# A longer hand-ordered opening: twelve pairs of groups instead of nine, another order behind W', and GpSimd from the fifth unit on

## Chip, cores, metric

The kernel runs on one core of one Trainium2 chip. The metric is the device time in microseconds of one execution. The core has five engines that run their own instruction queues in order: TensorE (PE in the profile, with its weight loads as PEld), VectorE (DVE), ScalarE (ACT), GpSimd (POOL) and SyncE (SP), which here only issues transfers.

## Reference

Three layers are computed one after the other on 2304 tokens:

```python
# q, k, v: (4, 8, 576, 64) float32
out = coarse_attention(mean4(q), mean4(k), mean4(v)) repeated 4 times
    + local_attention(q, k, v)          # |i - j| < 4
x = out as (2304, 512)
x = ((x @ w1) * (x @ w2)) @ w3 @ w_out  # w1, w2: 512x1024, w3: 1024x1024, w_out: 1024x512
h = x @ w_in                            # 512x2048
y = (h * sigmoid(h)) @ w_out2           # 2048x512
```

The weights arrive as float64 and are turned into float32 on the chip, in four integer and float steps per block.

## The kernel before

**Units, groups, slots.** Attention is cut into 16 units (one batch and two heads each). The product with w1 and w2 (called ab) is cut into 9 groups of 256 tokens and 8 blocks m of 128 columns; a pair (g, m) is two slots, one for w1 (w = 0) and one for w2 (w = 1). A slot is 12 matmuls of 128x128 by 128x256, in thirds a, b, c of four. Every three matmuls and every slot's end call `tick()`, so that a slot is four beats. There are 144 slots. Groups 0 and 1 need only units 0 to 3, and are the first 32 slots.

**W'.** w3 and w_out are multiplied into one matrix W' by 64 calls `p<half><gp><q>` of 128x128 by 128x512 in full float32; each is two MATMULs in the trace. Eight copies `wh<half><j>` bring it out of PSUM.

**The opening.** The list `OPENING` holds short names of steps; under `manual_schedule` every engine's queue gets its instructions in the order of that list. What stands there, by name (the last digit is the unit u, or the weight block m behind `w12_`):
- SP: `Lq`, `Lr`, `Lva`, `Lvb` (loads of q and k, of v for the coarse and the local part), `Lww12_m0/1` (weights), `Sc<g><m>` (store of a finished pair to DRAM)
- PE: `sd`, `s` (coarse and local scores), `td`, `tl` (transposes of the two probability tiles), `od`, `ol` (sums with v), `ab<g><m><w><third>`, `p...`
- ACT: `xd`, `x0`..`x2` (exponentials), `cd`, `cl` (copies of the transposes), `xh` (high half of x), `aw`, `hw` (first and fifth step of a weight block), `af` (copy of the first product of a pair), `wh`
- DVE: `md`, `mk`, `ml`, `rd`, `rl` (maxima, mask, inverses), `os`, `xf` (sums out of PSUM), `pq` (sums of q and k by four), `d2`, `d1`, `d3`, `lw` (steps of a weight block), `cf` (product of a pair)
- `nd`, `n0`..`n2` (norms of the probabilities), `pv0`, `pv1` (sums of v by four) and `xo` (low half of x): while `opening[0]` is true the norms run as small multiplications on ACT (line 374) and the others on DVE (lines 503, 510, 579). Behind the opening all of them run on GpSimd (the norm as one instruction, line 376).

PSUM has four banks for ab and W' (`mm`), two for transposes and sums (`T`), two for scores (`S`). `cf` has three buffers, `af` two, q/k, vr and vw two each, the probability tile `band` one, weight stages two.

**Behind the opening** only PE's order is written out by hand: slot after slot, with the units' steps taken from `table` when the beat comes (`TURN[u]`: transposes of u and scores of u+1; `SUMS[u]`: `ol`, x). The order on the other engines is made when the kernel is built. A background list `plan` decodes 16 more weight blocks (`bg_steps`) from slot 26 on, one every 21/4 slots; at its end the stage pools are closed (`open_y`). After slot 143 come the products with W', with w_in and with the last weights, all on PE.

In the version before, the opening ends with slot 17 (nine pairs, beat 72) and unit 6's exponentials; unit 6's turn is at beat 74, its sums at beat 88, unit 7's scores between. From slot 18 to the end of slot 23 (beat 96) three more pairs run under the table.

Of the kernel before, what the change touches and what calls it, by code (L numbers as in the profile page):

```python
# [11 lines left out]
ALU = mybir.AluOpType  # L12
# [3 lines left out]
NU = NB * NHP  # L16
# [36 lines left out]
n20 pv00 ao1 pv10 Lwt030 pq1 s1 cd00 cd10 tl00 tl10 d1o1 Lr1 cl00 sd1 cl10 d3o1 tl20 od0 Lwt031  # L53
cl20 md1 p010 os0 xd1 pq2 p011 Lq3 ao2 p012 d2o2 Lwt100 p013 rd1 mk1 nd1 p014 d1o2 Lwt101 d3o2 sd2
at02 d2t02 s2 Lww12_00 md2 p015 d1t02 p016 Lww12_01 d3t02 ao3 p017 ml1 ol0 Lq4 d1o3 x01 Lwt110 p020
pv01 x11 pv11 p021 d2o3 Lva1 x21 d3o3 p022 at03 p023 rl1 Lr2 d2t03 p024 n01 d1t03 n11 p025 d3t03
Lvb1 n21 p026 pq3 p027 Lwt111 p030 d2t10 at10 xf00 p031 Lww12_20 xf10 xh00 td01 d1t10 xh10 td11
cd01 d3t10 Lww12_21 p032 cd11 xd2 tl01 d2w12_0 tl11 p033 xo00 cl01 rd2 cl11 tl21 xo10 aw12_0 p034
mk2 ml2 od1 cl21 wh00 d1w12_0 p035 nd2 p036 os1 wh01 d3w12_0 p037 x02 ol1 wh02 wh03 pv02 p100 x12
Lva2 Lvb2 p101 x22 xf01 p102 xf11 hw12_0 rl2 td02 pv12 td12 n02 d2t11 Lr3 p103 n12 lw12_0 p104 n22  # L60
d2w12_2 sd3 xh01 xh11 xo01 cd02 s3 xo11 cd12 md3 tl02 at11 Lq5 tl12 pq4 p105 cl02 p106 cl12 aw12_2
d1t11 tl22 d3t11 od2 cl22 xd3 p107 os2 Lwt120 d1w12_2 p110 Lwt121 d3w12_2 sd4 rd3 ol2 Lww12_30
hw12_2 mk3 Lww12_31 ml3 nd3 p111 lw12_2 Lva3 Lvb3 x03 p112 xf02 p113 x13 xf12 pv03 td03 x23 d2t12
# [6 lines left out]
p137 wh12 Lva5 Lvb5 ab000a wh13 rd5 ab000b hw12_1 ab000c ab001a lw12_1 af00 nd5 ab001b ml5 ab001c  # L70
Lr6 ab100a cf00 Sc00 ol4 ab100b x05 xf04 xf14 ab100c xh04 x15 ab101a xh14 af10 x25 xo04 rl5 ab101b
xo14 ab101c ab020a cf10 Sc10 n05 n15 ab020b n25 pv05 ab020c pv15 Lva6 Lvb6 Lr7 ab021a af02 td05
cd05 ab021b td15 cd15 ab021c cf02 Sc02 ab120a pq6 tl05 cl05 ab120b tl15 cl15 ab120c ab121a aw12_5
af12 tl25 ab121b od5 cl25 os5 ab121c cf12 Sc12 ab030a d2w12_5 sd6 md6 ab030b d1w12_5 xd6 ab030c s6
Lq8 rd6 mk6 ab031a af03 ml6 ab031b nd6 d3w12_5 ab031c cf03 Sc03 ab130a x06 hw12_5 Lww12_60 ab130b
x16 lw12_5 Lww12_61 ab130c x26 rl6 ab131a af13 ol5 xf05 xf15 xh05 ab131b n06 n16 xh15 xo05 ab131c
n26 cf13 Sc13 xo15 ab010a aw12_4 d2w12_4 ab010b d1w12_4 ab010c ab011a af01 d3w12_4 ab011b hw12_4
ab011c cf01 Sc01 ab110a lw12_4 Lww12_70 ab110b Lww12_71 ab110c d2w12_6 aw12_6 ab111a af11 ab111b
d1w12_6 ab111c cf11 Sc11 ab050a d3w12_6 ab050b hw12_6 ab050c ab051a lw12_6 af05 ab051b aw12_7
ab051c d2w12_7 cf05 Sc05 d1w12_7 d3w12_7 hw12_7 lw12_7  # L80
""".split()


# [1 line left out]
def tile_model(ctx: ExitStack, tc: tile.TileContext, qk, vw, vr, w12, w3t, wo, wb, out):  # L85
    nc = tc.nc
# [78 lines left out]
    for g in range(4):  # L165
        mv = mask[QW * g:QW * g + QW]
        nc.gpsimd.affine_select(
            out=mv, in_=mv, compare_op=ALU.is_ge, fill=NEG, base=0,
# [3 lines left out]
            out=mv, in_=mv, compare_op=ALU.is_ge, fill=NEG, base=6,  # L172
# [140 lines left out]
    A = {}  # L313
    opening = [True]

    def side():
        return nc.vector if opening[0] else nc.gpsimd

    def load_qk(u):
        t = att.tile([P, 1158], F32, tag="qk", name=f"qk{u}")  # L320
# [29 lines left out]
    def unit_ops(u):  # L350
# [18 lines left out]
            nc.vector.reciprocal(out=sv, in_=sv)  # L369

        def norm(z, E, n, width, lo, hi):
            if opening[0]:
                for j in range(lo, hi):
                    nc.scalar.mul(E[:, j, :], E[:, j, :], z[:, NQB + j:NQB + j + 1])
            elif lo == 0:
                nc.gpsimd.tensor_tensor(
                    out=E, in0=E, op=ALU.mult,
                    in1=z[:, NQB:NQB + n].unsqueeze(2).to_broadcast([P, n, width]),
                )
# [120 lines left out]

        def pool_v0():
            r = A["vr", u][:HD]
            side().tensor_tensor(
                out=r[:, :, 0:2, :], in0=r[:, :, 0:2, :], in1=r[:, :, 2:4, :], op=ALU.add
            )

        def pool_v1():
            r = A.pop(("vr", u))[:HD]
            t = att.tile([HD, 2, P], F32, tag="vd", name=f"vd{u}", bufs=1)
            side().tensor_tensor(out=t, in0=r[:, :, 0, :], in1=r[:, :, 1, :], op=ALU.add)  # L510
            hold["vd"] = t

        def coarse_sums():
# [62 lines left out]

        def x_rest(h):
            for x, xf in x_parts(h):
                side().tensor_tensor(
                    out=x[:, 1], in0=xf, in1=x[:, 0].bitcast(F32), op=ALU.subtract  # L580
                )

# [2 lines left out]
        op("xd" + U, coarse_exps)  # L585
        op("rd" + U, lambda: inverse(hold["zd"], 3, 0.25))
        op("nd" + U, lambda: norm(hold["zd"], hold["Ed"], 3, SD, 0, 3))
        op("s" + U, local_scores)
        op("mk" + U, local_mask)
# [33 lines left out]
                fn()  # L623

    GAP = 4
    SUMS = {6: 88, **{u: 116 + 32 * (u - 7) for u in range(7, 16)}}
    TURN = {6: 74, 7: 102, **{u: SUMS[u] - 22 for u in range(8, 16)}}
    table = {}
    for u in range(6, NU):
        for when, names in (  # L630
            (TURN[u], f"pq{u + 1} td0{u} cd0{u} td1{u} cd1{u}"),
            (TURN[u] + GAP, f"tl0{u} cl0{u} tl1{u} cl1{u}"),
            (TURN[u] + 2 * GAP,
             f"tl2{u} od{u} cl2{u} os{u} pv0{u + 1} pv1{u + 1} sd{u + 1} md{u + 1} xd{u + 1} "
             f"rd{u + 1} nd{u + 1}"),
            (TURN[u] + 3 * GAP,
             f"s{u + 1} mk{u + 1} ml{u + 1} x0{u + 1} x1{u + 1} x2{u + 1} "
             f"rl{u + 1} n0{u + 1} n1{u + 1} n2{u + 1} Lq{u + 3} Lr{u + 3}"),
            (SUMS[u],
             f"ol{u} xf0{u} xh0{u} xo0{u} xf1{u} xh1{u} xo1{u} Lva{u + 2} Lvb{u + 2}"),  # L640
        ):
# [796 lines left out]
    with tc.manual_schedule(engines={E.PE, E.DVE, E.Activation, E.Pool, E.SP}):  # L1438
# [31 lines left out]
        for u in range(NUN):  # L1470
            t, p = divmod(u, 8)
# [98 lines left out]
```

## Time and profile before

| what | value |
|---|---|
| runs, median (lowest to highest) | 803.53 us (803.06 to 805.8), 3 runs |
| the profiled execution: time, span | 798.11 us, 796.3 us |
| PE busy | 784.8 us (99%), 7706 matmuls |
| DVE, ACT, POOL busy | 565.2 us (71%), 452.7 us (57%), 68.8 us (9%) |
| chain that ended last, by engine | PE 90%, DMA 3%, DVE 3%, ACT 2% |
| granted TensorE clock | full in all 40 slices |

The span is the time from the first to the last instruction of the profiled execution; 1.8 us of its time lie around the span. Matmuls are pipelined and their ends are modelled, so that a stretch in which PE is shown busy can still hold short waits: two starts compared say more than the busy time.

### The profile page before, as it was taken

Reading aid. Unit: us, or ns where it says so; the run is one execution under the profiler, and the core shown is the slowest. Engines: PE = TensorE matmul, PEld = TensorE weight load, DVE = VectorE, ACT = ScalarE, POOL = GpSimd, SP = SyncE. Lnnn points to the kernel's source line nnn. Section 1 sums busy time; section 2 is a strip of 40 time slices with the busy share of each in tenths; the row PEclk is TensorE's granted clock in tenths of the full one; section 3 lists DMA queues with packets and bytes.
Section 4 is the critical chain, followed back from the end, with each engine's and each line's share of the span. In section 5 each row is a group of like instructions: output and inputs, shape, how many; then the busy total and the mean of one; then the engine's idle time right before and its main releaser. Section 6 shows DMA issues by size and latency. Waiting matters only on the chain.

```text
span 796.3 us, 19454 instructions
## 1 busy us (share of the span) xinstructions
PE 784.8 (99%) x7706; PEld 730.4 (92%) x7706; DVE 565.2 (71%) x888; ACT 452.7 (57%) x1172; POOL 68.8 (9%) x90
## 2 busy tenths in 40 slices
PE   8999998999999999999999999999999999999998
PEld 5555687899999999999999999999999999999998
DVE  7989767676787664756889567435566798777771
ACT  6788876665565541534546568646677745444441
POOL 3000020443333310000000000000000000000000
PEclk9999999999999999999999999999999999999999
DMA  9978737778888778415384654454687965666640
GB/s 307 374 225 255 266 115 249 219 262 277 291 261 283 249 260 277 146 50 203 107 325 150 225 171 114 118 173 118 215 268 223 339 221 186 190 202 197 193 141 27
DMA packets 108138, 168.69 MB, mean 212 GB/s; under 512 B 16912, under 2 KB 78864, under 8 KB 107664
## 3 DMA queue, kind: packets, MB, share of 16 engines
q1 hardware_dynamic: 108048, 167.46, 65.2%
q8 instruction: 60, 0.98, 0.5%
q14 instruction: 30, 0.25, 0.1%
HBM read 115.00 MB, written 52.43 MB: 210 GB/s over the span
## 4 chain that ended last, share of the span: by engine, by line
PE 90%; DMA 3%; DVE 3%; ACT 2%; issue 1%; SPq 0%; DVEq 0%; ACTq 0%
PE ab L701 22%; PE yb L1158 11%; PE ox L1351 10%; PE hx L1212 9%; PE wp L662 6%; PE oy L1351 6%; PE hy L1212 6%; PE oz L1351 3%; PE hv L1212 3%; PE hz L1212 3%; PE ov L1351 3%; PE ol L541 2%; DMA qk<-qk 1%; PE s L434 1%; PE od L519 1%; PE td L459 1%
## 5 line engine op out<-in xcount | busy, mean ns | idle before, releaser
L701 PE MATMUL ab<-x,w_wA 128*128 128x256 f32 x864 | 108.5, 281 | 1.6 <-ACT af L712 1.2
L701 PE MATMUL ab<-x,w_wB 128*128 128x256 f32 x864 | 108.2, 281 | 0.0
L701 PEld LDWEIGHTS ab<-x,w_wA 128*128 128x128 f32 x864 | 101.9, 188 | 4.0 <-ACT af L712 1.6
L701 PEld LDWEIGHTS ab<-x,w_wB 128*128 128x128 f32 x864 | 101.8, 188 | 2.3 <-issue 1.6
L1158 PE MATMUL yb<-co,wy 128*128 128x384 f32 x504 | 87.5, 336 | 0.0
L1158 PEld LDWEIGHTS yb<-co,wy 128*128 128x128 f32 x504 | 87.3, 188 | 0.0
L1212 PE MATMUL hx<-yc,wc 128*128 128x384 f32 x432 | 83.1, 336 | 0.8 <-ACT u L1226 0.8
L1212 PEld LDWEIGHTS hx<-yc,wc 128*128 128x128 f32 x432 | 75.7, 188 | 1.2 <-ACT u L1226 1.2
L712 ACT COPY af<-ab 128x256 f32<-128x256 f32 x72 | 26.5, 368 | 62.5 <-PE ab L701 60.9
L662 PE MATMUL wp<-w_wo,w_w 128*128 128x512 f32 x128 | 60.0, 602 | 0.1
L1212 PE MATMUL hy<-yc,wc 128*128 128x384 f32 x288 | 57.7, 336 | 0.0
L1351 PE MATMUL oy<-wo,S 128*128 128x256 f32 x432 | 51.9, 276 | 0.0
L1351 PE MATMUL ox<-wo,S 128*128 128x256 f32 x432 | 51.9, 276 | 0.0
L1194 ACT ACTIVATE c<-c 128x384 f32<-128x384 f32 x96 | 48.0, 526 | 6.8 <-DVE c L1124 6.0
L1212 PEld LDWEIGHTS hy<-yc,wc 128*128 128x128 f32 x288 | 50.6, 188 | 0.0
L1351 PEld LDWEIGHTS oy<-wo,S 128*128 128x128 f32 x432 | 50.3, 188 | 0.0
L1351 PEld LDWEIGHTS ox<-wo,S 128*128 128x128 f32 x432 | 50.3, 188 | 0.0
L359 ACT ACTIVATE band<-band,sml 128x38 f32<-128x38 f32 x144 | 44.9, 317 | 4.7 <-DVE sml L450 4.7
L717 DVE TENSOR_TENSOR cf<-ab,af 128x256 f32<-128x256 f32 x72 | 30.2, 419 | 21.0 <-PE ab L701 10.2
L662 PEld LDWEIGHTS wp<-w_wo,w_w 128*128 128x128 f32 x128 | 22.4, 190 | 21.1 <-issue 19.1
L1218 ACT COPY p<-hx 128x384 f32<-128x384 f32 x24 | 11.5, 480 | 42.5 <-PE hx L1212 42.5
L1023 ACT CAST co<-cb 128x768 fp32r<-128x768 f32 x32 | 25.7, 836 | 17.2 <-DVE cb L1007 13.8
(188 smaller groups left out, 1451.9 us busy)
## 6 DMA issues: line engine op xcount, KB each, us to landing
gd<-c SPq DMA_DIRECT2D x96, 192.0 KB
sw<-wb SPq DMA_DIRECT2D x32, 512.0 KB
qk<-qk SPq DMA_DIRECT2D x16, 579.0 KB
big<-gd SPq DMA_DIRECT2D x18, 512.0 KB
A<-gd SPq DMA_DIRECT2D x18, 512.0 KB
S<-gd SPq DMA_DIRECT2D x17, 512.0 KB
cb<-cd SPq DMA_DIRECT2D x10, 768.0 KB
st<-w SPq DMA_DIRECT2D x14, 512.0 KB
```

What stands on the lines that cost most here:

```text
L359: nc.scalar.activation(E[:, j, :], src[j], AF.Exp, bias=z[:, j:j + 1], scale=scale, accum_out=z[:, NQB + j:NQB + j + 1],)
L541: nc.tensor.matmul(acc[h][r, c0:c0 + QW], lhsT=v[k, sub, c, r], rhs=ET[k, c, q0:q0 + QW], start=True, stop=True,)
L662: nc.tensor.matmul(wp_ps[half, j], lhsT=w3v[:, k, j * P:(j + 1) * P], rhs=wov[:, k, :], start=(gp == 0 and k == 0), stop=(gp == 3 and k == 1),
L701: nc.tensor.matmul(acc[:, :GW], lhsT=wv[:, i, w, kk, :], rhs=X[g, kk][:, j, :], start=(n == 0), stop=(n == 11),)
L712: mark(nc.scalar.copy(af, C.pop(("ab", g, m, 0))[:, :GW]))
L717: nc.vector.tensor_tensor(out=cf, in0=C.pop(("ab", g, m, 1))[:, :GW], in1=C.pop(("af", g, m)), op=ALU.mult)
L1023: nc.scalar.copy(d[:, 0], src)
L1158: nc.tensor.matmul(acc[e], lhsT=WY[o][:, a, 2 * g + k, c0:c0 + P], rhs=y[:, b, k, :], start=(n < 2 and (a, b) == (0, 0) and i in (0, 1, 2, ...
L1194: nc.scalar.activation(v, v, AF.Silu)
L1212: nc.tensor.matmul(acc, lhsT=WC[s][:, a, c, kt * P:(kt + 1) * P], rhs=y[:, b, kt, :], start=(n == 0 and i in (0, 1, 2, 4)), stop=(n == 5), ...
L1218: nc.scalar.copy(p1, X_)
L1351: nc.tensor.matmul(acc, lhsT=A[:, a, p * P:(p + 1) * P], rhs=B_[name, p // 4][:, b, p % 4, :], start=(p == 0 and q == 0 and name in begin) ...
```

## The change

The opening goes on to slot 23 (twelve pairs, `NSTATIC = 24`), with another order of everything from W''s last eight calls on. It now also holds unit 6's turn and sums and unit 7's scores and exponentials. Norms, `pv` and `xo` go by the unit's number: units 0 to 4 on ACT and DVE, units 5 and up on GpSimd, inside the opening too. The table starts at unit 7 (its turn one beat earlier); the background list starts at slot 32 instead of 26, one block every 39/8 slots, and ends one slot later.

```diff
@@ OPENING, old end (its first 359 names stay as they are)
-x04 d1t13 ol3 x14 d2t13 d3t13 x24 sd5 Lva4 Lvb4 pv14 s5 Lww12_50 rl4 Lr5 xf03 aw12_1 p130 Lq7
-d2w12_1 Lww12_51 td04 xf13 n04 p131 d1w12_1 n14 d3w12_1 td14 n24 p132 md5 cd04 p133 xh03 cd14 xo03
...
-x16 lw12_5 Lww12_61 ab130c x26 rl6 ab131a af13 ol5 xf05 xf15 xh05 ab131b n06 n16 xh15 xo05 ab131c
-n26 cf13 Sc13 xo15 ab010a aw12_4 d2w12_4 ab010b d1w12_4 ab010c ab011a af01 d3w12_4 ab011b hw12_4
-ab011c cf01 Sc01 ab110a lw12_4 Lww12_70 ab110b Lww12_71 ab110c d2w12_6 aw12_6 ab111a af11 ab111b
...
@@ OPENING, new end
+x14 d2t13 d3t13 x24 sd5 Lva4 Lvb4 pv14 s5 Lww12_50 rl4 Lr5 xf03 aw12_1 p131 md5 pq6 xh03 Lww12_51
+p130 p134 p133 n14 xo03 p135 p137 wh10 xf13 td04 td14 n04 Lq7 ab000a d2w12_1 cd04 cd14 p132 d1w12_1
+tl04 xd5 n24 d3w12_1 od4 ab000b s6 ab000c p136 cl04 os4 tl14 wh11 wh13 ab001a ab001b Lr6 tl24 af00
+wh12 ab001c ab100a Lq8 cl14 d2w12_5 mk5 xh13 Lva5 ml5 Lww12_40 ab101a cl24 cf00 ol4 xo13 ab020a
...
+nd6 ab011a lw12_5 ab111c ab010a xf05 ab010b ab011b aw12_6 rl6 ab131a ab010c cf11 n06 td06 xf15 Lr9
+ab131b n16 n26 tl06 af01 Lww12_70 Lww12_71 cd06 Lva8 ab050a cl06 Sc12 xh15 tl16 d2w12_6 ab011c
+lw12_4 Lvb8 d1w12_6 cf01 tl26 mk7 ml7 ab131c cf13 ab050b cl16 td16 cl26 sd7 xh05 ab150a cd16 xo05
+od6 ab150b ab150c aw12_7 ab050c Lvb6 ab051a ab051b md7 ab051c ab151a xd7 pq8 ab151b x17 pv17 af15
+rd7 Sc11 af05 os6 d2w12_7 d3w12_6 cf05 Lr8 ol6 x07 xf16 xo15 x27 Sc01 Sc13 nd7 ab040a xh16 ab151c
+xf06 cf15 rl7 hw12_6 Sc05 Lva7 ab040b Lvb7 ab040c ab140a d1w12_7 ab141a Sc15 xo16 ab140b d3w12_7
+ab041a ab140c xh06 ab141b lw12_6 af04 n17 ab141c ab041b af14 ab041c cf14 cf04 Sc04 hw12_7 lw12_7 n07
+Sc14 xo06 n27
@@
-    def side():
-        return nc.vector if opening[0] else nc.gpsimd
+    def side(u):
+        return nc.vector if u < 5 else nc.gpsimd
@@ norm()
-            if opening[0]:
+            if u < 5:
@@
-    SUMS = {6: 88, **{u: 116 + 32 * (u - 7) for u in range(7, 16)}}
-    TURN = {6: 74, 7: 102, **{u: SUMS[u] - 22 for u in range(8, 16)}}
-    table = {}
-    for u in range(6, NU):
+    SUMS = {u: 116 + 32 * (u - 7) for u in range(7, NU)}
+    TURN = {u: SUMS[u] - (22 if u > 7 else 15) for u in range(7, NU)}
+    table = {96: ["Lva8 Lvb8"]}
+    for u in range(7, NU):
@@
-    table[72] = ["pv06 pv16 Lr8 Lva7 Lvb7"]
@@
-    NSTATIC = 18
+    NSTATIC = 24
@@
-    starts = [26 + (21 * n) // 4 for n in range(len(units))]
+    starts = [32 + (39 * n) // 8 for n in range(len(units))]
```

The calls `side()` in `pool_v0`, `pool_v1` and `x_rest` become `side(u)`.

## Rows read from the trace of the kernel before

**Rows 1.** The page, busy tenths of the span's 40 slices: PE.
```profile
PE   8999998999999999999999999999999999999998
```
**Rows 2.** Windows: stretch, length, busy us of each engine, clock, DMA share, GB/s.
```profile
24.00:84.86 60.86, 60.81 (x785) 32.80 (x786) 54.78 (x102) 50.24 (x185) 0.00 (x0) 1.00 0.85 276
84.86:144.68 59.82, 55.95 (x753) 47.82 (x746) 42.72 (x84) 42.70 (x163) 9.56 (x8) 1.00 0.64 207
144.68:287.17 142.49, 142.47 (x2253) 132.53 (x2256) 107.32 (x231) 78.99 (x329) 49.21 (x58) 1.00 0.81 265
```
**Rows 3.** Waits of PE from 84.86 to 144.68: total us, times, longest.
```profile
PE ab L701 <- ACT af L712: 1.2, 2, 0.8
PE tl L489 <- ACT EdT L478: 0.8, 1, 0.8
PE tl L489 <- ACT ET L496: 0.7, 1, 0.7
PE ol L541 <- ACT Ed L359: 0.7, 1, 0.7
PE ab L701 <- DVE cf L717: 0.4, 1, 0.4
```
**Rows 4.** Windows of PE between the `ol` of successive units, first and last of six.
```profile
172.55:189.41 16.86, 16.86 (x275) 1.00 0.90 310
...
256.18:272.61 16.43, 16.43 (x275) 1.00 0.77 231
```
**Rows 5.** Timeline of PE: start, us, line, tiles, count.
```profile
151.54 0.52 PE L392 MATMUL sd<-qkd 64*128 64x144 f32 x4
...
152.37 1.68 PE L701 MATMUL ab<-x,w_wA 128*128 128x256 f32 x12
153.98 0.85 PE L434 MATMUL s<-qk 64*32 64x38 f32 x72
154.76 0.97 PE L701 MATMUL ab<-x,w_wA 128*128 128x256 f32 x6
```
**Rows 6.** The chain that ended last: start, us, what.
```profile
34.97 8.78 PE wp L662 x20
...
288.45 69.58 PE ab L701 x612
...
462.01 8.15 DMA gd<-c
```
**Rows 7.** Timeline of ACT ahead of two waits of PE.
```profile
121.15 1.41 ACT L374 ACTIVATE band<-band,sml 128x38 f32<-128x38 f32 x6
...
123.42 1.12 ACT L206 ACTIVATE dec<-st 128x1024 f32<-128x1024 f32 x1
124.45 0.35 ACT L712 COPY af<-ab 128x256 f32<-128x256 f32 x1
```
**Rows 8.** Lines of POOL over the span, by form: count, busy us, mean ns.
```profile
L503 POOL TENSOR_TENSOR vr<-vr 72x512 f32<-72x512 f32 x10 | 14.1, 1413 | 102.2 <-DMA vr<-vr 101.8 <-issue 0.4
...
L510 POOL TENSOR_TENSOR vd<-vr 72x256 f32<-72x256 f32 x10 | 9.8, 975 | 55.7 <-PE od L519 46.7 <-DMA vr<-vr 9.0
L376 POOL TENSOR_TENSOR Ed<-Ed,smd 128x432 f32<-128x432 f32 x9 | 8.2, 906 | 27.2 <-ACT af L712 14.8 <-DVE smd L369 8.3 <-DMA vr<-vr 4.0
L376 POOL TENSOR_TENSOR band<-band,sml 128x342 f32<-128x342 f32 x9 | 6.9, 765 | 22.0 <-DVE sml L369 22.0
L579 POOL TENSOR_TENSOR x<-xf,x 128x192 fp32r<-128x192 f32 x6 | 4.1, 682 | 2.2 <-ACT x L575 2.2
```
**Rows 9.** Instructions of line 223 on DVE: ns least, median, most.
```profile
L223 DVE SCALAR_TENSOR_TENSOR dec<-dec,sw x16: 1208/1215/2193, 149.9 to 306.5; 128x1024 int32<-128x1024 int32 x16
L223 DVE SCALAR_TENSOR_TENSOR dec<-dec,st x7: 1216/1225/1682, 63.1 to 135.7; 128x1024 int32<-128x1024 int32 x7
```
**Rows 10.** Timeline of POOL and of DVE at 115 us.
```profile
114.53 1.28 POOL L503 TENSOR_TENSOR vr<-vr 72x512 f32<-72x512 f32 x1 [2.69 <-DMA vr<-vr]
...
115.22 1.68 DVE L223 SCALAR_TENSOR_TENSOR dec<-dec,st 128x1024 int32<-128x1024 int32 x1
```

More of the change, by code (lines that the diff above doesn't have):

```diff
@@ L52 @@
 Lwo21 at01 rl0 p004 p005 nd0 d1t01 Lwt020 p006 d3t01 Lwt021 n00 Lwo30 td00 n10 d2o1 td10 Lwo31 p007
[L53 to L63, printed above, removed]
@@ L64 @@
-td13 p114 pv13 at12 md4 Lr4 p115 rl3 xh02 d1t12 s4 xh12 n03 d3t12 p116 Lq6 n13 p117 xo02 Lwt130 n23
-xo12 Lwt131 p120 d2w12_3 cd03 cd13 pq5 p121 xd4 tl03 tl13 pv04 aw12_3 p122 rd4 p123 cl03 d1w12_3
-cl13 nd4 tl23 d3w12_3 od3 p124 cl23 os3 Lww12_10 hw12_3 mk4 p125 Lww12_11 ml4 at13 p126 lw12_3 p127
-x04 d1t13 ol3 x14 d2t13 d3t13 x24 sd5 Lva4 Lvb4 pv14 s5 Lww12_50 rl4 Lr5 xf03 aw12_1 p130 Lq7
-d2w12_1 Lww12_51 td04 xf13 n04 p131 d1w12_1 n14 d3w12_1 td14 n24 p132 md5 cd04 p133 xh03 cd14 xo03
-tl04 tl14 p134 xh13 cl04 xo13 cl14 tl24 p135 wh10 cl24 od4 mk5 wh11 xd5 p136 Lww12_40 Lww12_41 os4
@@ L70 @@
[L70 to L75, printed above, removed]
@@ L76 @@
-x16 lw12_5 Lww12_61 ab130c x26 rl6 ab131a af13 ol5 xf05 xf15 xh05 ab131b n06 n16 xh15 xo05 ab131c
-n26 cf13 Sc13 xo15 ab010a aw12_4 d2w12_4 ab010b d1w12_4 ab010c ab011a af01 d3w12_4 ab011b hw12_4
-ab011c cf01 Sc01 ab110a lw12_4 Lww12_70 ab110b Lww12_71 ab110c d2w12_6 aw12_6 ab111a af11 ab111b
-d1w12_6 ab111c cf11 Sc11 ab050a d3w12_6 ab050b hw12_6 ab050c ab051a lw12_6 af05 ab051b aw12_7
-ab051c d2w12_7 cf05 Sc05 d1w12_7 d3w12_7 hw12_7 lw12_7
+n20 pv00 ao1 pv10 Lwt030 pq1 s1 cd00 cd10 tl00 tl10 d1o1 Lr1 cl00 sd1 cl10 d3o1 tl20 od0 Lwt031 cl20
@@ new lines @@
+md1 p010 os0 xd1 pq2 p011 Lq3 ao2 p012 d2o2 Lwt100 p013 rd1 mk1 nd1 p014 d1o2 Lwt101 d3o2 sd2 at02
+d2t02 s2 Lww12_00 md2 p015 d1t02 p016 Lww12_01 d3t02 ao3 p017 ml1 ol0 Lq4 d1o3 x01 Lwt110 p020 pv01
+x11 pv11 p021 d2o3 Lva1 x21 d3o3 p022 at03 p023 rl1 Lr2 d2t03 p024 n01 d1t03 n11 p025 d3t03 Lvb1 n21
+p026 pq3 p027 Lwt111 p030 d2t10 at10 xf00 p031 Lww12_20 xf10 xh00 td01 d1t10 xh10 td11 cd01 d3t10
+Lww12_21 p032 cd11 xd2 tl01 d2w12_0 tl11 p033 xo00 cl01 rd2 cl11 tl21 xo10 aw12_0 p034 mk2 ml2 od1
@@ new lines @@
+cl21 wh00 d1w12_0 p035 nd2 p036 os1 wh01 d3w12_0 p037 x02 ol1 wh02 wh03 pv02 p100 x12 Lva2 Lvb2 p101
+x22 xf01 p102 xf11 hw12_0 rl2 td02 pv12 td12 n02 d2t11 Lr3 p103 n12 lw12_0 p104 n22 d2w12_2 sd3 xh01
+xh11 xo01 cd02 s3 xo11 cd12 md3 tl02 at11 Lq5 tl12 pq4 p105 cl02 p106 cl12 aw12_2 d1t11 tl22 d3t11
+od2 cl22 xd3 p107 os2 Lwt120 d1w12_2 p110 Lwt121 d3w12_2 sd4 rd3 ol2 Lww12_30 hw12_2 mk3 Lww12_31
+ml3 nd3 p111 lw12_2 Lva3 Lvb3 x03 p112 xf02 p113 x13 xf12 pv03 td03 x23 d2t12 td13 p114 pv13 at12
@@ new lines @@
+md4 Lr4 p115 rl3 xh02 d1t12 s4 xh12 n03 d3t12 p116 Lq6 n13 p117 xo02 Lwt130 n23 xo12 Lwt131 p120
+d2w12_3 cd03 cd13 pq5 p121 xd4 tl03 tl13 pv04 aw12_3 p122 rd4 p123 cl03 d1w12_3 cl13 nd4 tl23
+d3w12_3 od3 p124 cl23 os3 Lww12_10 hw12_3 mk4 p125 Lww12_11 ml4 at13 p126 lw12_3 p127 x04 d1t13 ol3
+x14 d2t13 d3t13 x24 sd5 Lva4 Lvb4 pv14 s5 Lww12_50 rl4 Lr5 xf03 aw12_1 p131 md5 pq6 xh03 Lww12_51
+p130 p134 p133 n14 xo03 p135 p137 wh10 xf13 td04 td14 n04 Lq7 ab000a d2w12_1 cd04 cd14 p132 d1w12_1
+tl04 xd5 n24 d3w12_1 od4 ab000b s6 ab000c p136 cl04 os4 tl14 wh11 wh13 ab001a ab001b Lr6 tl24 af00
@@ new lines @@
+wh12 ab001c ab100a Lq8 cl14 d2w12_5 mk5 xh13 Lva5 ml5 Lww12_40 ab101a cl24 cf00 ol4 xo13 ab020a
+aw12_5 rd5 pv05 x25 x15 ab021a Lww12_41 xf14 Sc00 Lvb5 ab020b xf04 d1w12_5 ab100b nd5 ab100c x05
+af10 td05 ab101b ab101c rl5 hw12_1 td15 d3w12_5 ab020c xh04 cf10 ab030a ab030b Lva6 cd15 Lww12_60
+ab021b n05 ab021c n15 n25 cd05 pv15 tl05 lw12_1 xo04 tl15 af02 cl05 ab030c af03 ab031a ab031b ab031c
+cl15 Lr7 sd6 Sc10 pv06 hw12_5 ab120a tl25 cf02 d2w12_4 Sc02 Lww12_61 cf03 md6 aw12_4 Sc03 xd6 ab121a
+ab110a pq7 ab120b cl25 xh14 ab121b ab130a ab130b mk6 od5 pv16 s7 ab110b ab110c ml6 x26 os5 pv07 x06
@@ new lines @@
+ab120c d1w12_4 ab121c ol5 d3w12_4 af12 ab130c ab111a Lq9 af11 rd6 x16 cf12 af13 hw12_4 ab111b xo14
+nd6 ab011a lw12_5 ab111c ab010a xf05 ab010b ab011b aw12_6 rl6 ab131a ab010c cf11 n06 td06 xf15 Lr9
[3 more added lines that the diff above has]
+rd7 Sc11 af05 os6 d2w12_7 d3w12_6 cf05 Lr8 ol6 x07 xf16 xo15 x27 Sc01 Sc13 nd7 ab040a xh16 ab151c
@@ L502, in pool_v0 @@
             r = A["vr", u][:HD]
-            side().tensor_tensor(
+            side(u).tensor_tensor(
                 out=r[:, :, 0:2, :], in0=r[:, :, 0:2, :], in1=r[:, :, 2:4, :], op=ALU.add
@@ L509, in pool_v1 @@
             t = att.tile([HD, 2, P], F32, tag="vd", name=f"vd{u}", bufs=1)
-            side().tensor_tensor(out=t, in0=r[:, :, 0, :], in1=r[:, :, 1, :], op=ALU.add)
+            side(u).tensor_tensor(out=t, in0=r[:, :, 0, :], in1=r[:, :, 1, :], op=ALU.add)
             hold["vd"] = t
@@ L578, in x_rest @@
             for x, xf in x_parts(h):
-                side().tensor_tensor(
+                side(u).tensor_tensor(
                     out=x[:, 1], in0=xf, in1=x[:, 0].bitcast(F32), op=ALU.subtract
```

## Prediction, made blind

> **What bounds the kernel now.** I read the page first, then windows, then the waits of one engine, then its order in time. By the slices [rows 1] PE is busy nine tenths or more nearly everywhere; the slices with an eight are the first, the seventh (about 119 to 139 us) and the last. So the end is set by PE's own queue, and a change of order can only win back time in which PE stands still. The windows [rows 2] say where that is. From 24.00 to 84.86 us PE is idle for 0.05 us, although DVE is at 54.78 of 60.86 us (90%): that is the first part of the hand-written order, which stays. From 144.68 to 287.17 us, under the table, it is idle for 0.02 us. Between them, from 84.86 (the first `p130`) to 144.68 us (the end of slot 23: the 24th of 42 products that begin at 141.89), 59.82 us hold 55.95 busy: 3.87 us of idling. This is just the stretch whose order is rewritten. By beat 96 both versions have done the same work on PE: eight calls of W', 24 slots, transposes and sums of units 4 to 6, scores of units 6 and 7. So the question is by how much the stretch shrinks; everything behind it is shifted.
>
> The waits [rows 3] name the causes: twice `ab` for an `af` (1.2 us), once for a `cf` (0.4), a transpose for a copy on ACT twice (0.8 and 0.7), `ol` for an exponential (0.7). All are banks of PSUM that come free late because the releasing instruction stands behind others in its queue. The order on ACT shows one [rows 7]: `af` starts at 124.45 us, behind a weight's first step at 123.42 and behind norms that began at 121.15, while the product it copies had ended before.
>
> **What the stretch costs without waits.** Six units under the table take 16.68 us each (first 16.86, last 16.43; 172.55 to 272.61 us is 100.06) [rows 4], each with 96 products and one of everything that a unit needs on PE. Three of them have the 288 products of 24 slots and three units, but one pair of scores too many: `sd` 0.83 us (151.54 to 152.37) and `s` 0.78 (153.98 to 154.76) [rows 5], 1.61 together. W' adds 16 MATMULs of 0.439 us (20 in 8.78) [rows 6], 7.02 us. Sum: 3 x 16.68 - 1.61 + 7.02 = 55.45 us. The old order needs 59.82, so 4.37 us are to be had, of which 3.87 show as idling; the rest hides in modelled ends.
>
> **What the new order adds on PE.** I counted in the two lists how often the stream of `ab` is broken by other work: 16 runs of `ab` before, 20 after (W' is left and taken up again, and unit 6's small transposes stand between single thirds). Twelve products between two breaks took 1.61 us (152.37 to 153.98) [rows 5], against 12 x 0.1137 = 1.36 in the long run (612 in 69.58) [rows 6]: at most 0.25 us for a break, nothing at least. Four more cost 0 to 1.0; I take 0.6, since the row comes from just such breaks but with a longer neighbour.
>
> **What it removes and moves.** For units 5 and 6 the norms leave ACT: 12 small multiplications each, six of which took 1.41 us [rows 7], so 24 x 0.235 = 5.6 us. ACT falls from 42.70 us [rows 2] to about 37 in a stretch of about 56. DVE loses `pv05`, `pv15` and unit 5's `xo`, and stays below its 42.72 us [rows 2]. POOL gets unit 5's `pv` (1.41 and 0.98), two norms (0.91 and 0.77) and `xo` (at most three of 0.68), 6.1 us, and unit 6's norms, 1.7 [rows 8]: 9.56 + 7.8 = 17.4 us. By sums none of the three is the bound: 37, 43 and 17 of 56. `pv06`, `pv16`, unit 6's `xo` and unit 7's work ran on POOL already.
>
> In-order queues can still stall with such sums, so I followed the new list by hand, each step starting when its queue and its inputs are ready. The places with the least room:
> - The start. `ab000a` takes the bank of W''s first sum. Its copy `wh10` can run after `p134`, the third call, and three calls of 0.88 us and `td` lie before `ab000a`. No wait. On ACT `wh10` makes `n04`, `cd04`, `xd5` wait for `p134`, about 1 us; `s6` needs the bank that `xd5` frees, which comes one step earlier.
> - SP. `Lq8` waits for `s6`, which reads the old buffer; behind it stand `Lva5`, `Lww12_40` and `Lww12_41`, so they go out some 10 us into the stretch, and their users (`ol5`, `aw12_4`) come at about 31 and 24. `Lww12_60` waits for `d3w12_5` and has over 10 us until `aw12_6`. `Lr9` and `Lva8` now stand ahead of `Lr8` and `Lva7`; unit 8 needs them only under the table. These transfers cost nothing while that room lasts; without it `aw12_6` would hold up `af01` and `cd06` behind it on ACT.
> - Unit 6's turn. Each transposed tile needs the bank of the tile two before it. Between `tl06` and `tl26` PE has two thirds (0.45 us each by the long run [rows 6]) and `tl16`, about 1.2 us, for a copy on ACT; the old order had such a wait at 0.8 and at 0.7 us [rows 3]. About 0.5 us of room.
> - The ring of three `cf`. `cf15` reuses the buffer of `cf01`, and the store `Sc01` stands behind `Lr8`, which waits for `pv17`, which waits for `od6`. After `od6` PE has ten thirds and `ol6`, about 6 us, to `cf15`'s product, and five more thirds until PE needs that bank. `pv17` (0.98 us [rows 8]) and two issues leave about 6.5 us for the store to land. The longest landing in the chain, of another store, is 8.15 us [rows 6]: the stall is 0 to 1.7. I take 0, as most of that row is a queue of other transfers.
>
> Two places have less than a microsecond of room, so I leave 0.3 us for small waits (bounds: 0, and 3.0 as in the second rival). Order of the later engines, table and background list: the unit's turn moves one beat, the background's sixteen blocks run in 78 slots instead of 84, so DVE, at 75% behind the stretch [rows 2], gets about 3% more work per slot; PE idled 0.02 us there, and the cover is a quarter of DVE's time. `open_y` comes one slot later, and its loads have the slots up to 143. I cost these at 0 (bounds 0 and 0.5).
>
> **Sum.** 4.37 - 0.6 - 0.3 = 3.5 us less. Against the profiled execution's own time: 798.11 - 3.5 = 794.6. The median of the runs, 803.53, lies 5.4 above that execution; with the same distance the prediction is 800.0 us (0.44% less). About 0.3%, 2.4 us, is what can be told from no change here.
>
> **Where GpSimd's share speaks against it.** At 114.53 us POOL began an addition of 1.28 us, until 115.81; a DVE step of 1024 columns that began at 115.22 took 1.68 us [rows 10], against a median of 1.22; the background's sixteen such steps go up to 2.19 [rows 9]. So the two engines hold each other up: here by 0.46 us. Yet behind the stretch POOL worked 49.21 us, next to 107.32 of DVE, and PE idled 0.02 [rows 2]. The Trainium skill (SBUF — State Buffer, Who interferes with whom) says that a VectorE instruction with two SBUF inputs and a GpSimd instruction that reads SBUF exclude each other, the loser waiting for the whole instruction. By that rule the trace agrees, as the row at 115.22 waits for about the end of POOL's.
>
> **The rivals.**
> 1. *The order holds* (my forecast): gain of 2.4 to 4.4 us, 799.1 to 801.1, likeliest 800.0. For it: the first 60 us of the same hand-written kind run with 0.05 us of idling at a fuller DVE [rows 2]. Chance 0.68.
> 2. *The waits move*: the banks of the transposes in units 5 and 6 come late once more, each with a pair of waits of 0.8 and 0.7 [rows 3]: 3.0 us, less the 0.3 already counted. 800.0 + 2.7 = 802.7 us, no difference. For it: half a microsecond of room at `tl26`. Against it: ACT has 5.6 us less to do, and the norms that held up `af` are gone. Chance 0.24; it also takes the store of `cf01`.
> 3. *DVE is held up by POOL and becomes the bound*: if all of POOL's 17.4 us came on top of DVE's 42.7, DVE would need 60.1 us without a gap. It also waits for PE's results (17.1 us of the old stretch were idle [rows 2]); with half of that left, 60.1 + 8.5 = 68.6, which is 8.8 more than 59.82: 812.3 us, slower. It decides when over 62.2 - 42.7 - 8.5 = 11 of 17.4 us, 63%, fall on DVE. Against it: 0.46 of 1.28 in the one row [rows 10], and the quiet stretch behind. Chance 0.08.
>
> That the change does not do what it says I can exclude: the order is written out for each engine.
>
> **Range and chances.** Below, 4.37 us and no extra break give 799.2; the six units may hide small waits of their own, and medians here scatter by 0.5, so 798.0. Above, rival 2 gives 802.7, and with the same scatter and the half microsecond of the background 803.6. What is left out is rival 3 and the odd case. Faster by over 0.3%: 0.68; within: 0.24; slower: 0.08.
>
> **What would show it.** Right: from 84.86 us on (nothing before it moves) PE reaches its 288th product at about 141.2 instead of 144.7 us, with under 0.7 us of idling between, no wait of `ab` for `af`, and the rest shifted. ACT's norms of line 374 fall by 24 and POOL rises by about 7.8 us. Wrong: waits of `tl`, `td`, `od` or `ol` for `cd` and `cl` (rival 2); DVE instructions of lines 211, 217, 223 and 300 well over their medians and PE waiting for `cf` (rival 3); or idling behind beat 96, where I expect none.

## The result, and the profile after

The changed kernel takes 792.32 us (median of 6, 791.41 to 797.79) against 803.29 for the kernel before, run beside it (6, 797.84 to 805.8): a ratio of 0.9891, interval 0.9852 to 0.993. It is faster, and by more than the forecast range allowed: 800.0 was forecast, with 798.0 as the low end. In a second comparison the same two kernels stood closer: 794.0 against 800.24, ratio 0.9912 (0.9881 to 0.9944), a distance of 6.2 instead of 11.0 us. What follows shows that some 6 us belong to the change. The rest of the first distance is put down to a condition of single executions that either kernel can be in.

First the slices of the page after, PE, to be laid beside [rows 1]: the dip of the seventh slice is gone. (The eight in the second slice belongs to the waits of the first 25 us, below.)

```profile
PE   8899999999999999999999999999999999999998
```

Then the windows after, the same three parts as [rows 2], cut where the changed kernel reaches the same points of its work (the first of the last eight calls of W', the end of the 288th product, the beginning of the last `ol`); the columns are length, busy us of PE, PEld, DVE, ACT and POOL, clock, DMA share, GB/s.

```profile
24.00:86.33 62.33, 62.28 (x801) 33.78 (x799) 56.13 (x104) 50.34 (x186) 0.00 (x0) 1.00 0.84 269
86.33:141.26 54.93, 54.93 (x751) 48.05 (x746) 45.46 (x77) 38.21 (x140) 21.90 (x20) 1.00 0.71 215
141.26:282.44 141.18, 141.18 (x2253) 131.73 (x2254) 110.42 (x227) 79.02 (x326) 47.64 (x54) 1.00 0.82 269
```

The rewritten stretch takes 54.93 instead of 59.82 us and has no idling at all. Its beginning comes 1.47 us later, though nothing ahead of it was changed: in this execution PE waited 2.6 us for the loads of `qk`, against 0.7 in the one before. And the stretch under the table is 1.31 us shorter (141.18 against 142.49). The waits of PE, over the whole run, are only those of its first 25 us; none of the five of [rows 3] is left:

```profile
PE s L438 <- DMA qk<-qk: 2.6, 2, 2.0
PE sd L409 <- DVE qkd L345: 1.4, 1, 1.4
PE spare L152 <- DVE zero L148: 1.3, 1, 1.3
```

In the profiled executions the distance is therefore made up as follows: +1.47 at the start, -4.89 in the stretch, -1.31 under the table and about -1.1 in a later stage, where the execution before had a wait of 0.8 us (`hx` for a copy on ACT) that this one lacks: -5.8 us, from a span of 796.3 to one of 790.5. The medians are 11 apart. So there were two questions: which part of the change removes the waits, and where the other 5 us come from.

### The profile page after: what moved, and what is told of

The parts are those of the page before. It is cut to its first block, busy times and chain, and to the rows that moved or that the text cites. A ratio compares the mean times of both kernels' runs of the same rounds, so it can differ in the third digit from the quotient of the medians.

```text
span 790.5 us, 19444 instructions
## 1 busy us (share of the span) xinstructions
PE 781.7 (99%) x7706; PEld 729.6 (92%) x7706; DVE 574.1 (73%) x883; ACT 448.2 (57%) x1148; POOL 79.5 (10%) x99
## 4 chain that ended last, share of the span: by engine, by line
PE 96%; DMA 2%; DVE 0%; SPq 0%; issue 0%; ACT 0%
PE ab L704 26%; PE yb L1161 11%; PE ox L1354 10%; PE hx L1215 9%; PE wp L665 6%; PE hy L1215 6%; PE oy L1354 6%; PE hv L1215 3%; PE hz L1215 3%; PE oz L1354 3%; PE ov L1354 3%; PE ol L545 3%; DMA qk<-qk 1%; PE s L438 1%; PE td L463 1%; PE od L523 1%
```

## The experiments

### Where executions of one kernel differ: the kernel before, twice

`b_again1` and `b_again2` are the kernel before without an edit.

> The kernel before, unchanged, for a second trace. The profiled execution of before (798.11 us) lay 5.4 us below the median of its runs. Theory A (a part that varies lies outside the rewritten stretch): an execution near 803 us shows the same 59.8 us between the first call p130 and the 288th product of ab, and some 5 us more elsewhere, at the start or in the stages with the last weights. Theory B (the old order is sensitive to when transfers land): the extra 5 us lie in the rewritten stretch, as more idling of PE than 3.87 us.

> The kernel before once more, a third trace; the same two readings as for the second. Should one of the traces be near 798 and one near 803 us, the difference between the two says where the 5 us are.

They took 798.89 and 806.54 us. Up to the first product of the last stage they are 1.2 us apart (it starts at 622.1 and 623.3 us). The rest is in the last stage, in the time from product to product. Windows of PE of `b_again1`, then of `b_again2` (length, busy us and MATMULs, clock, DMA share, GB/s):

```profile
680.00:700.00 20.00, 20.00 (x179) 1.00 0.61 190
```

```profile
680.00:700.00 20.00, 20.00 (x172) 1.00 0.59 185
```

Both are busy throughout at a granted clock of 1.00, yet one does 179 products and the other 172. 24 products take 2.72 us (113.3 ns each) in the one and 2.83 (117.8 ns, 4% more) in the other. The timeline of `b_again2` shows where the short pitch ends, at a wait of PE for a copy on ACT (start, us, idle before and its releaser):

```profile
653.71 2.88 PE L1351 MATMUL ox<-wo,S 128*128 128x256 f32 x24
656.43 2.88 PE L1351 MATMUL oy<-wo,S 128*128 128x256 f32 x24
659.76 1.45 PE L1351 MATMUL ox<-wo,S 128*128 128x256 f32 x10 [0.45 <-ACT u2o L1364]
```

Starts are 2.72 us apart before the wait; behind it the pitch is 2.83 up to the end of the run. The chain of waits tells why the copy was late: a transfer landed late and a split on ACT stood ahead of the copy.

```profile
651.03 7.29 DMA A<-gd
...
658.39 1.05 ACT A L1294
659.44 0.28 ACT u2o L1364
```

The span ends at 804.8 us, so 145 us are left at that point, and 4 parts in 104 of these are 5.6 us, for a wait of 0.45 us; the last stage as a whole took 6.4 us longer. So the two executions differ by a pitch, hardly by the opening. The distance of 5.4 us between the profiled execution and the median, on which the prediction had put its sum, has just the size of the long pitch. The short pitch shows with the new opening too (the changed kernel's profiled execution), and so does the long one (`after_b` and `norm_pool`, below).

### The order alone

`order_only` has the new order, with the norms of units 5 to 7 on ACT and their sums of v and low halves on DVE, by the old rule for the opening. It is not quite the old share of the engines: the opening now reaches further, so unit 6's sums and low halves and unit 7's work, which had run on GpSimd behind the old opening, come to DVE and ACT with it.

```
-        return nc.vector if u < 5 else nc.gpsimd
+        return nc.vector if opening[0] else nc.gpsimd
...
-            if u < 5:
+            if opening[0]:
```

> The new order alone: norms, sums of v and low halves of x of units 5 to 7 run on ScalarE and VectorE in the opening, as before. If the order wins the time (my theory), PE has no wait of ab for af or cf and the time is within 2 us of the changed kernel, 792 to 795 us; the norms come back to ACT (36 small multiplications of 0.235 us, 8.5 us), which has about 37 of 55 us to do. If the move to GpSimd wins it, the waits of PE for af come back and the time is near before, 800 us or more.

Measured: 795.69 us (9 runs), ratio 0.9931 (0.9906 to 0.9957). Its windows of the rewritten stretch, and its waits:

```profile
85.31:142.56 57.25, 55.76 (x751) 47.98 (x746) 42.49 (x87) 45.27 (x173) 2.58 (x2) 1.00 0.67 201
```

```profile
PE ab L704 <- issue: 2.1, 1, 2.1
PE tl L493 <- ACT EdT L482: 1.1, 1, 1.1
PE tl L493 <- ACT EdT L476: 0.4, 1, 0.4
```

The transposes wait for their copies on ACT twice, at 108.68 and 126.74 us, 1.5 us together: the second rival as it was forecast, but only where the norms stay on ACT. ACT's 45.27 us are 2.6 more than before; these are nine norms of unit 7, which start at 135.20 us, behind both waits, so the waits are not their doing. (The wait of 2.1 us comes at 158 us, behind the stretch, and shows no releaser.)

### GpSimd's share alone

`pool_only` has the old order, but the work goes to GpSimd from unit 5 on:

```
-    def side():
-        return nc.vector if opening[0] else nc.gpsimd
+    def side(u):
+        return nc.vector if u < 5 else nc.gpsimd
...
-            if opening[0]:
+            if u < 5:
```

> The old order with the units from 5 on handled by GpSimd in the opening too. If the order wins the time: PE still waits for cf and for the banks of the transposes, about 2 to 3.9 us of idling in the stretch, and the time is within 2 us of before. If GpSimd wins it: the idling falls below 1 us and the time is 4 us or more below before.

Measured: 799.94 us (12 runs), ratio 0.9992 (0.9961 to 1.0023): no difference that can be told. In the profiled execution the stretch took 58.19 us, with these windows and waits:

```profile
89.25:147.44 58.19, 55.49 (x753) 47.69 (x746) 42.03 (x79) 37.47 (x140) 17.48 (x18) 1.00 0.69 209
```

```profile
PE tl L489 <- ACT EdT L472: 1.1, 1, 1.1
...
PE ol L541 <- ACT Ed L359: 0.6, 1, 0.6
PE ab L701 <- ACT af L712: 0.4, 1, 0.4
```

ACT has its 5 us less to do (37.47 against 42.70), and there are still three waits for it, 2.1 us together, where [rows 3] has five, 3.4: in the old order a smaller sum of ACT's work does not clear them. So in the stretch each half of the change wins some of the time and neither all of it: 57.25 and 58.19 us, between 59.82 before and 54.93 after, in one profiled execution each.

### The order, and of GpSimd's share only the norms

`norm_pool` is the changed kernel with the sums of v and the low halves of units 5 to 7 on DVE, and their norms on GpSimd:

```
-        return nc.vector if u < 5 else nc.gpsimd
+        return nc.vector if opening[0] else nc.gpsimd
```

> The new order with only the norms on GpSimd; sums of v and low halves of x of units 5 to 7 on VectorE in the opening. If ACT's queue was what the new order could not bear without GpSimd, this is as fast as the changed kernel, within 1 us, and 2.5 to 3.5 us faster than the new order alone (795.69 us). If VectorE was it, it stays with the new order alone.

Measured: 794.57 us (7 runs), ratio 0.992 (0.9889 to 0.9951), the same as the whole change beside it. Its window of the stretch:

```profile
85.43:140.36 54.93, 54.93 (x751) 48.05 (x746) 45.12 (x87) 37.63 (x140) 9.41 (x8) 1.00 0.69 209
```

54.93 us without idling, as in the changed kernel. So the gain of the stretch is the order together with the norms; the other work that went to GpSimd brings nothing. It does not even relieve DVE, which is busy 45.12 us with 87 instructions here and 45.46 with 77 in the changed kernel. Beside `order_only` DVE has the same 87 instructions, POOL 6.83 us more (9.41 against 2.58), and DVE is busy 2.63 us longer (45.12 against 42.49). That would be 39% of what POOL got, near the 0.46 of 1.28, 36%, of the prediction's one row [rows 10]. But it is one execution against one, and DVE's busy time of this stretch scatters by 1.9 us (42.7 to 44.6) in five executions of the old opening, so the share is an indication and no price.

### The changed kernel again

`after_b` is the changed kernel without an edit.

> The changed kernel again, beside the kernel before on one chip. Theory: the change itself is worth about 6 us (execution against execution: 798.11 to 792.25), and the 11 us between the first medians come from the kernel before, whose executions stand some at 797 to 801 us and some at 803 to 809; the slower ones have a slower pitch of the last stage. Then the fastest and the lower quartile of both kernels lie 5.5 to 6.5 us apart, whatever the medians do. Rival: the change also keeps executions out of the slower pitch; then nearly all of its runs stay below 795 while the kernel before has a third or more at 803 and over.

Measured: 794.0 us (8 runs from 791.3 to 799.14), ratio 0.9912 (0.9881 to 0.9944). Its profiled execution, 797.74 us, reaches the last stage when the first one did (615.4 and 615.6 us), keeps the short pitch there up to 651 us, and then runs at the long one to its end:

```profile
680.00:700.00 20.00, 20.00 (x172) 1.00 0.60 189
```

So the changed kernel has the long pitch too; in the first comparison it fell on fewer of its executions than of the kernel before, by their times.

### The background's spacing

`bg_dense` is the kernel before with the closer spacing of the background's blocks:

```
-    starts = [26 + (21 * n) // 4 for n in range(len(units))]
+    starts = [26 + (39 * n) // 8 for n in range(len(units))]
```

> The kernel before with only the background list closer, one block every 39/8 slots from slot 26 on. Behind the 288th product the changed kernel needed 141.2 us to the last ol against 142.5. If the spacing of the background did that, this kernel is 1.0 to 1.3 us faster than before there, and its units take about 16.5 us instead of 16.7; if it did not, the time stays within 0.5 us and the units at 16.7.

Measured: 802.61 us (12 runs), ratio 1.0019 (0.9988 to 1.005). It gained nothing, and its profile has a wait that the kernel before had not, of a transpose for POOL, beside the known ones:

```profile
PE tl L489 <- POOL band L376: 1.2, 1, 1.2
```

So the 1.31 us under the table do not come from the spacing. From the start of the 289th product to the last product of `ab`, `bg_dense` took 213.2 us, five executions with the old opening and the old spacing took 212.6 to 214.5 us, seven with the new opening 211.8 to 215.9, with the same mean of 213.4 to 0.1: this term is scatter.

### A wait made on purpose in the last stage

`forced_wait` is the changed kernel with set 1 of the last stage in another order, so that a product has to wait for the bank that the one before it used:

```
-            order = OPS
+            order = OPS if n != 1 else ("A11", "A12", "A22", "S2", "S1", "S4", "S3")
```

> The changed kernel with one more wait of PE: in the second of the last stage's nine sets the products S1 and S4 stand next to each other, so that PE waits for ACT's copy of their bank, some 0.5 to 0.7 us. If a wait can lock PE into the slower pitch (24 products in 2.83 us instead of 2.72), the runs rise by up to 0.6 + 6 us, to 798 or 799, in many or all executions; if a wait costs only itself, they rise by 0.7 us at most, to 793.

Measured: 797.85 us (12 runs), ratio 0.9981 (0.9949 to 1.0013). Six runs lie within 794.97 to 796.94 and six within 798.76 to 804.71. The profiled one is of the lower sort: it has the wait, and the short pitch behind it.

```profile
651.84 2.99 PE L1354 MATMUL oy<-wo,S 128*128 128x256 f32 x24 [2.63 <-ACT p5o L1365]
654.66 2.88 PE L1354 MATMUL ox<-wo,S 128*128 128x256 f32 x24
657.38 2.88 PE L1354 MATMUL ox<-wo,A 128*128 128x256 f32 x24
```

That every wait brings the long pitch is thereby refuted: a wait of 2.63 us did not, one of 0.45 did. A wait can turn the pitch over, and does not always.

### Products that set the pitch

If the pitch can be set by hand, the scatter can be taken out of the comparison. `reset512` puts one extra product, 512 columns wide, at the head of each of sets 1 to 8 of the last stage; `reset256` a pair of 256 columns; `before_reset` is the kernel before with the edit of `reset512`. The extra products write a bank that is begun anew directly behind them.

```
+            if n > 0:
+                nc.tensor.matmul(wide, lhsT=A_[n, "A11"][:, 0, :P], rhs=A_[n, "A11"][:, 0, :512],
+                                 start=True, stop=True, skip_group_check=True)
```

(The expectations speak of sets 1 to 5 and of five products; there are eight, 1.8 us.)

> The changed kernel with one extra product of 512 columns at the head of each of the last stage's sets 1 to 5 (its result is overwritten); five of them cost about 1.1 us. Theory: the upper executions of both kernels owe their 5 to 6 us to the slower pitch of the last stage (24 products in 2.83 us instead of 2.72), which begins at a short wait of TensorE and holds because the weight loads no longer run ahead of the products; a wide product lets them get ahead again, so the pitch ends at the next set, no execution loses more than about 1.5 us to it, and the runs lie between 792.5 and 795 with the median near 793.5. Rival: the pitch has nothing to do with how far the loads are ahead; then it holds through the wide products, the runs are spread over 792.5 to 800 and the median is 1 us above the changed kernel's 794.0, about 795.

> The changed kernel with a pair of extra products of 256 columns, as set 0 has them already, at the head of the last stage's sets 1 to 5 (overwritten, some 1.1 us in all). Theory of the loads that have to get ahead: products of the same width as all others give them no room, so the slow pitch stays where it has begun, runs from 792.5 to 800, median near 795. Rival: any break in the row of products between the stage's sets ends the slow pitch; then 792.5 to 795, median near 793.5, as with the wide product.

> The kernel before with the same wide product at the head of sets 1 to 5. Theory: its upper executions come down by 5 us for a price of 1.1 us, runs 798 to 801, median about 799.5, and the distance to the changed kernel with the same product is the opening's own 6 us. Rival (the pitch is not ended): 798 to 808, median about 801.5, 1 us above the kernel before.

Measured: `reset512` 800.87 us (12 runs, 799.18 to 805.16; ratio 0.9999, 0.9978 to 1.002), `reset256` 798.74 (12 runs, one of them at 2754.66, the others 796.7 to 801.62; 0.9979, 0.996 to 0.9998), `before_reset` 807.33 (6 runs, 805.91 to 808.08; 1.0075, 1.0051 to 1.0099). None of the forecast times held: the wide product does not end the long pitch. The chain of waits of `reset512`, with the wide product as the row of 0.23 us:

```profile
655.53 0.23 PE ox L1352
655.77 2.83 PE ox L1360 x24
```

All sets behind a wide product run at 2.83, in `before_reset` too, and by their times (not one run within 7 us of the lowest of the same kernel without the edit) so did every other execution of the two. The pair turns the pitch over each time, here from 2.72 to 2.83 and back (chain of `reset256`; it goes on so to the end, set for set):

```profile
654.70 2.72 PE ox L1360 x24
657.42 0.23 PE ox L1352 x2
657.65 2.83 PE ox L1360 x24
...
674.61 2.83 PE ox L1360 x24
677.43 0.24 PE ox L1352 x2
677.67 2.73 PE ox L1360 x24
```

With the pitch held long in both, the kernels are 807.33 - 800.87 = 6.46 us apart (lowest runs: 6.73), without the pitch in the difference; the expectation of `before_reset` had named 6 for the opening alone. Resampled from these runs the distance lies between 5.2 and 7.7 us.

### The pitch held short

`pin_apart` uses both findings: the wide product at the head of set 2 (long, as it should be from either pitch), the pair at the head of set 3 (over to short). `before_pin` is the same on the kernel before. `pin_near` has the pair directly behind the wide product, at the heads of sets 2 and 4.

```
+        if n in (2,):      # pin_near: (2, 4)
+            nc.tensor.matmul(wide, ...)          # 512 columns
+        if n in (3,):      # pin_near: (2, 4)
+            for _ in range(2):
+                nc.tensor.matmul(X_, ...)        # 256 columns
```

> The changed kernel with one wide product (512 columns) at the head of set 2 of the last stage and a pair of products of 256 columns at the head of set 3, all overwritten. Theory (the wide product always leaves the slow pitch behind, the pair turns the pitch over): set 2 runs in 19.8 us (24 products in 2.83) in every execution, all sets from 3 on in 19.0 (2.72). Cost of the three products and of set 2's pitch 1.2 us on top of the lowest runs of the changed kernel, 791.3: runs within 792 to 795.5, median about 793.5. Rival (the pitch follows waits and chance, not these products): runs from 792 to 800, median about 794.5 to 795.

> The changed kernel with the wide product and the pair directly behind it, at the heads of sets 2 and 4 (0.9 us of products). If the pitch is settled within a few products of the wide one, the pair turns it to the fast one in sets 2 to 8: runs 792 to 794.5, median about 793. If it takes a longer row of products to settle, the pair does not act as in a slow set, sets 2 to 8 stay at 2.83 us and the runs lie near 798.

> The kernel before with the products of pin_apart: the wide one at the head of set 2, the pair at that of set 3. Theory: the upper executions vanish here too, runs 798 to 802, median about 800, and the distance to pin_apart is the opening alone, 6 to 6.5 us, as between the two kernels whose pitch was held slow (807.33 and 800.87). Rival: runs 798 to 808 and a median of 801 to 803.

Measured: `pin_apart` 795.17 us (6 runs, 792.78 to 797.2; ratio 0.9906, 0.9869 to 0.9942), `before_pin` 801.31 (12 runs, 799.41 to 803.4; 0.9997, 0.9972 to 1.0022), `pin_near` 797.48 (12 runs, 794.71 to 801.92; 0.9938, 0.9911 to 0.9966). The chain of `pin_apart` shows the steps as expected:

```profile
654.78 2.72 PE ox L1366 x24
657.50 0.23 PE ox L1352
657.73 2.83 PE ox L1366 x24
...
674.69 2.83 PE ox L1366 x24
677.52 0.24 PE ox L1358 x2
677.75 2.73 PE ox L1366 x24
```

The upper executions are gone in the kernel before, where they can be counted: the kernel before ran from 797.94 to 807.96 beside them (23 runs), with the pitch set from 799.41 to 803.4. The medians are 801.31 - 795.17 = 6.14 us apart, between 4.6 and 8.9 when the six and twelve runs are resampled, which still spread over 4 us each. The medians themselves came out 1.3 to 1.7 above their expectations, where the rivals had put theirs; so what speaks for the theory are the steps in the traces, one execution of each kernel, and the missing upper executions, and not the medians. In `pin_near` the wide product and the pair led to the long pitch at set 2, where they came directly behind a wait, and to the short one at set 4. So the pair does not act in every case as in a settled row of products, and neither of the two expectations for it held.

## Why the prediction was wrong, step by step

**The base: the step that failed most.** The step "with the same distance the prediction is 800.0 us" carried the 5.4 us between the profiled execution and the median of before over to the changed kernel. That distance has the size of the long pitch, which by their times five of six executions of the kernel before had in the first comparison; its profiled one had not. The three executions behind the 803.53 were all at 803 or over, as are only 17 of 90 in the four later comparisons, whose median is 800.3 (two outliers, 809.6 and 814.88, left out). The changed kernel's median lay 0.07 us above its profiled execution (792.32 and 792.25) there, and its executions reach up to 799.14 in the other comparison. It is a property of single executions, so it could not be added as a constant; the range should have held both cases. Without the 5.4 us the forecast's own sum gives 794.6; of the 7.7 us between forecast and result this step makes 5.35.

**The sum of the stretch: right in its mechanism, too small in size.** 3.5 us were forecast, 59.82 to 56.35. The stretch after took 54.93, so 4.89 beside the profiled execution. The small waits, 0.3, came to nothing, as PE does not idle. The other two terms, 55.45 for the stretch without waits and 0.6 for four more breaks of `ab`, are 1.1 us too high together. The trace does not part them: 55.45 alone is half a microsecond over what was measured, and with three of the shortest of the six units, 16.43 us [rows 4], the same sum is 3 x 16.43 - 1.61 + 7.02 = 54.70, which leaves 0.2 for the breaks. Either way the mean of the units of [rows 4] was too long for a stretch without waits, as the prediction had suspected in its range alone. The new order takes this time in every execution: from the first of the eight calls to the 289th product, 54.93 to 54.99 us in seven profiled executions with the whole new opening (five of them of kernels whose last stage was edited). The old order took 59.88, 60.11, 60.43, 60.86 and 61.29 in five (without `bg_dense`): mean 60.51. The profiled execution of before was the best of them, and the change is worth 5.6 us here, 0.6 more than that one execution shows.

**The places with the least room: right.** None of the four that were followed by hand (the bank of W''s first sum, SP's queue, unit 6's turn, the ring of three `cf`) shows a wait. The 288th product ended at 141.26 us, and 141.2 was forecast, but this is two errors that cancel: the stretch began 1.47 us later and was 1.4 us shorter than forecast. In the five and seven executions its beginning lies at 84.80 to 86.16 and at 85.42 to 86.69 us; why it is later by some 0.7 on average, where the work ahead of it is the same, stays open.

**The second rival, waits that move to the transposes: refuted for the change, right for the order alone.** `order_only` has just these, 1.5 us. What removes them are the norms taken from ACT, as the prediction had argued against this rival.

**The third rival, DVE held up by POOL: refuted.** ACT's norms fell by 24 (1172 to 1148 instructions), as forecast. POOL rose by 12.3 us in the stretch (9.56 to 21.90), not by 7.8. It got 12 instructions more there, and the prediction had counted nine: the other three, a norm of unit 7 and two low halves, had run behind the stretch before. Over the whole run POOL has just nine more (90 to 99) and is busy 10.7 us longer (68.8 to 79.5). So its instructions are also longer than the prediction had them, as the groups of POOL's instructions in the stretch after show (busy, mean ns, idle before; the first mixes shapes) beside the 0.77 us of the prediction's norm and the 0.68 of its `xo` [rows 8]:

```profile
L583 POOL TENSOR_TENSOR x<-xf,x 128x192 fp32r<-128x192 f32 (+2 forms) x6 | 5.5, 922 | 2.5 <-ACT x L579 2.5
L380 POOL TENSOR_TENSOR band<-band,sml 128x342 f32<-128x342 f32 x3 | 3.4, 1132 | 4.3 <-DVE sml L373 4.3
```

DVE lost seven instructions and was still busy longer, 45.46 against 42.72 us, below which the prediction had it. More executions bear this out: 42.7 to 44.6 us with 83 or 84 instructions in five with the old opening, 45.2 to 46.3 with 77 to 81 in seven with the new one. So the two engines do hold each other up. What refutes the rival is that PE has no wait for DVE in the stretch in any of the seven: at 45 to 46 of 55 us DVE is not the bound.

**Behind beat 96: no loss, and no gain that holds.** 0 was forecast. In the first profile 1.31 us were won, and in the mean of the executions nothing. Three of the seven with the new opening have a late wait there of 1.5 to 1.8 us (the last section), as has `order_only`; the kernel before has some of 0.5 to 1.05. Whether the new order makes them more frequent is not settled.

**Together.** With the pitch held alike, 6.1 to 6.5 us separate the kernels by their medians; 5.6 of them are the stretch. In the five and seven profiled executions the last stage begins 5.1 us earlier on average (0.7 lost at the beginning, 5.6 won in the stretch, 0.1 lost up to the end of `ab`, 0.4 won between it and the last stage): 6.4 in the four without the late wait, 3.3 in the three with it. So the microsecond or so between the 5.1 and the medians may hang on how often that wait comes, which was not measured. The 11.0 of the first comparison hold some 4.5 to 4.9 more, by the times from the long pitch in five of six executions of the one kernel and in at most two of six of the other. That this was chance is argued, from both kernels having both pitches later, and not shown: only 25 of those 90 later executions of the kernel before reach 802.2 us, the lowest of those five, so that a condition of the first comparison alone is not excluded. None of the variants was faster than the changed kernel itself.

## What to carry to other kernels

Before a sum of terms is set on a median, find out what separates the profiled execution from that median: profile the unchanged kernel two or three times and compare stage by stage. Where an extra few products can hold such a condition alike in both versions, it drops out of the difference: 6.1 and 6.5 us here, where two comparisons without it gave 11.0 and 6.2. And where two engines' queues stall each other, reckon order and load together: here the order alone left waits for ACT, the lighter ACT alone left waits for the order, and only both removed all of them; work moved from VectorE to GpSimd beyond that gave VectorE no time back.

## What the runs showed of the hardware

**Two pitches at one clock.** Products of 128x256 with nothing to wait for follow each other at 113.3 or at 117.8 ns with the granted clock at 1.00 in both, and keep to either until something turns it over: some short waits, a wide product (to the long one, or it stays there), a pair of products (over, from either; directly behind a wide product it did so in one of two places of `pin_near`). What in the engine makes it is open: the guess in the expectations, weight loads that no longer run ahead, would have a wide product do the opposite.

**A short wait can cost as much again.** Behind some waits of 0.7 to 2 us the granted clock falls for a while to the lower of its two levels (1.2 instead of 2.4 GHz). In `reset256` PE waited 1.52 us at 203.37 for something not shown; the windows around it:

```profile
200.00:204.00 4.00, 2.48 (x82) 1.00 1.01 325
204.00:208.00 4.00, 4.00 (x33) 0.58 0.63 235
208.00:212.00 4.00, 4.00 (x37) 0.99 0.88 269
```

At 0.58 in 4.00 us, 42% of these, 1.7 us, are lost on top of the wait. `pin_near` has the same behind its wait of 1.72 us at 250.45 (0.88 and 0.69 in the two slices), and `bg_dense` behind one of 0.66 at 141.01 (0.79 and 0.79 in the slices from 140 us), while `pin_apart`'s wait of 1.77 at 251.70 and `order_only`'s of 2.13 left the clock at 1.00. In the old opening it happened within the stretch itself, behind the wait of a transpose in `b_again1`:

```profile
136.12 0.29 PE L489 MATMUL tl<-ident,band 128*38 128x128 f32 x1 [1.09 <-ACT ET L496]
```

```profile
136.00:140.00 4.00, 3.81 (x31) 0.77 0.98 360
140.00:144.00 4.00, 4.00 (x155) 0.80 0.64 214
```

In `pool_only` it came near the start, behind a wait of 1.95 us for the load of `qk`. It cost (0.47 + 0.38) x 4 = 3.4 us, most of what its stretch began late (89.25 us):

```profile
24.00:28.00 4.00, 4.00 (x24) 0.53 1.04 411
28.00:32.00 4.00, 4.00 (x7) 0.62 1.02 327
```

So a wait that is removed is worth its own length and now and then 1.7 us more, which the profile of one execution may not show.
